# Moving an early output projection into a wait, widening narrow matmuls, splitting one load and adding fill matmuls, in a decode step that is bound by its loads

## The chip, the cores, the metric

One core of a Trainium2 chip runs the whole program. The metric is device time in microseconds (us) of one execution. The kernel before takes 672.7 us (median of three executions). A time of an execution is about 1.8 us more than the span that its profile shows, and the profile's times count from the start of the span.

Words used below: a *value unit* is one 4 MB load of the value cache (two heads of one batch) and the 32 matmuls on it; a pass is one batch, with four key units and then four value units; the *tail* is what follows the key units of the last batch. *Half clock* and *full clock* are a granted TensorE clock of 0.50 and 1.00 in the profile.

## The reference

A transformer block for one new token in each of 8 batches: adaptive layer norm, attention with 32 query heads over a cache of 8 key/value heads by 8192 positions, output projection, layer norm, MLP with squared ReLU.

```python
mod = (silu(c) @ w_mod).reshape(8, 6, 1, -1)          # sa, ca, ga, sb, cb, gb
h = layernorm(x) * (1 + ca) + sa
q = (h @ wq) ...                                       # 32 heads of 128
p = softmax(q k^T * 128**-0.5);  o = p v               # caches: 8 x 8 x 8192 x 128 bf16, twice
x = x + ga * (o @ wo)                                  # wo: 4096 x 512
h = layernorm(x) * (1 + cb) + sb
r = relu(h @ w1 + b1);  x = x + gb * ((r * r) @ w2 + b2)   # 512 x 1792, 1792 x 512
```

## The kernel before

Every large load goes through one queue, in the order of need, into a ring of four 4 MB slots. In the tail the order is: third value unit; last value unit in four pieces (2, 1, 0.5, 0.5 MB); the 1 MB of output weights that belong to the last unit; first MLP weights (1.75 MB); second MLP weights (1.5 and 0.25 MB). In all timelines below TensorE's matmuls come in the order of the program. The parts that matter, with cuts:

```python
for p in range(NP):                       # last batch: value units 0, 1, 2, then the last
    if not lastu:
        for m in range(32):  # matmul bank(p) += Pm(32 cols) x values(512 cols), 4 column groups
        ...                                # copy, 4 selecting matmuls, normalise -> oTn
    else:
        ...                                # issue loads of wo (last part), W1, W2
        # early output projection of units 0..2
        for hl in range(REP):
            for j in range(4): ...         # 16 permuting matmuls -> pP, then copied to oP
        for f in range(FT): ...            # 14 bias matmuls into hT_ps; 2 into yN_ps
        for g in range(6):
            for j in range(4):
                for k in range(KT):        # 96 matmuls, 8 moving columns each
                    op("tensor", ... e.matmul(attn_ps[:, k, :], wo_sb[:, 4*g+j, k*128:(k+1)*128],
                                              oP[:, j, g, :], ...), [t, d_woe])
        ...                                # last unit: 24 matmuls, then 2 x 16 with 8 columns ("direct")
        for x in range(8):
            for k in range(KT): ...        # last projection: 32 matmuls, waits for d_wo
...                                        # residual, layer norm (with 4 and 14 fill matmuls) -> hbT
for hh in range(2):                        # first MLP layer: 56 matmuls of 8 columns
    for f in range(7*hh, 7*(hh+1)):
        wcol = lambda k, f=f: W1v[:, k, :].rearrange("p (q f) -> p f q", f=FT)[:, f, :]   # step of 14
        for k in range(KT): ...  e.matmul(hT_ps[hh][:, f % 7, :], wcol(k), hbT[:, k, :], ...)
for f in range(FT):                        # second layer: 28 matmuls of 256 columns, wait for d_w2
    ...
```

`pe_fill(n)` issues n matmuls of 128 columns on an identity whose result nobody reads; they are meant to keep the clock up.

## Time and profile before

| | us |
|---|---|
| time, median | 672.71 |
| span of the profiled execution | 670.8 |
| last weights land (issue time plus time to landing) | about 665 |
| end of the second MLP layer | 667.9 |
| half clock in the tail | 629.6 to 633.0, 643.2 to 646.6, and from 650.05 to the end |

From the page of the kernel before: the span, then three rows of 40 equal slices (granted clock in tenths, busy share of the DMA engines in tenths, GB/s), then the bytes read.

```profile
span 670.8 us, 15868 instructions
...
PEclk9998985799869986799578987599777998699875
...
DMA  9999999999999999999999999999999999999995
...
GB/s 376 430 420 426 432 432 432 425 434 434 432 436 423 434 434 432 436 424 432 434 436 432 428 425 434 436 436 432 422 432 434 436 436 424 428 434 438 436 391 210
...
HBM read 283.66 MB, written 0.01 MB: 423 GB/s over the span
```

The DMA row is 9 from the first slice to the last but one. The program is its loads: 283.66 MB at 423 GB/s. What can shrink without fewer bytes is only what happens after the last bytes, so everything below is about the last 45 us.

The DMA view of the kernel before, for three loads of the tail (size, and us from issue to landing), and the timeline's lines of their issue (start, duration, engine, source line). Issue plus time to landing gives 656.4 us for the output weights, 660.9 for the first MLP weights and 664.5 for the larger part of the second.

```profile
wo_sb<-in_A_wo_dram SPq DMA_DIRECT2D x1, 1024.0 KB, 29.8
...
ring<-in_B_w_dram SPq DMA_DIRECT2D x1, 1792.0 KB, 24.6
...
ring<-in_B_w_dram SPq DMA_DIRECT2D x1, 1536.0 KB, 15.2
```

```profile
626.55 0.42 SPq L560 DMA_DIRECT2D wo_sb<-in_A_wo_dram  x1
...
636.33 12.95 SPq L562 DMA_DIRECT2D ring<-in_B_w_dram  x1
...
649.32 2.50 SPq L565 DMA_DIRECT2D ring<-in_B_w_dram  x2
```

The timeline of the kernel before, TensorE's lines of the tail (start us, duration us, engine, source line, operation, operands, count, and in brackets the idle time before it and what ended that).

```profile
634.38 1.91 PE L536 MATMUL PS<-ring,Pm 128*32 128x512 bf16 x32 [0.54 <-DVE rinv L517]
...
637.27 1.91 PE L536 MATMUL PS<-ring,Pm 128*32 128x512 bf16 x32
...
643.54 3.41 PE L536 MATMUL PS<-ring,Pm 128*32 128x512 bf16 x32 [3.31 <-DMA ring<-in_A_v_cache_dram]
...
648.55 1.01 PE L583 MATMUL PS<-ONE,b_row 1*128 1x8 bf16 x14
...
649.69 2.69 PE L594 MATMUL PS<-oP,wo_sb 128*128 128x8 bf16 x96
...
652.31 2.75 PE L610 MATMUL PS<-ring,Pm 128*32 128x512 bf16 x24
...
656.87 1.02 PE L627 MATMUL PS<-oTn,wo_sb 128*128 128x8 bf16 x32 [0.29 <-DVE oTn L622]
...
661.30 3.51 PE L665 MATMUL PS<-hbT,ring 128*128 128x8 bf16 x56
...
664.74 3.15 PE L676 MATMUL PS<-ring,hidT 128*8 128x256 bf16 x28
```

The first two value units take 1.91 us each, the third 3.41: that is the clock. Before the third TensorE idled 3.31 us for a load. The block of early projection (L594, 96 matmuls, 28 ns each) lies between the third and the last unit. The first MLP layer (L665) takes 63 ns for each matmul, the output projection's (L627) 32, at the same clock and of the same shape.

The clock in the same stretches, from the windows view of the kernel before (window, length, busy us and count of each engine, granted clock, DMA share, GB/s):

```profile
core 0: us, PE busy (x) PEld busy (x) DVE busy (x) ACT busy (x) POOL busy (x), PEclk, DMA share, GB/s
633.00:643.00 10.00, 4.67 (x74) 2.26 (x74) 2.47 (x8) 1.49 (x2) 0.00 (x0) 1.00 0.99 424
643.00:646.50 3.50, 2.96 (x28) 1.12 (x32) 0.00 (x0) 0.00 (x0) 0.00 (x0) 0.53 0.98 414
650.00:660.00 10.00, 8.91 (x198) 6.34 (x196) 1.96 (x8) 0.00 (x0) 0.00 (x0) 0.50 1.07 402
660.00:670.00 10.00, 7.89 (x99) 6.41 (x96) 2.30 (x9) 0.90 (x3) 0.00 (x0) 0.50 0.25 99
```

TensorE is "busy" 8.91 of 10 us from 650 to 660 and still has half the clock: 164 of the 198 matmuls in that stretch stream 8 columns.

### The profile page before, as it was taken

What the parts mean: (1) busy time and instruction counts of PE and PEld (TensorE: products, weight loads), DVE (VectorE), ACT (ScalarE), POOL (GpSimd) and SP (SyncE); (2) the same over time, 40 slices, a digit from 0 to 9 for tenths busy, and PEclk for the clock granted to TensorE, in tenths of its full rate; (3) what the DMA queues carried; (4) which work ended last, traced back from release to release, by engine and by line L of the source; (5) the groups of instructions that cost most, each with busy time, mean ns of one, the idle gap of its engine ahead of it and who ended that gap; (6) DMA issues with size and microseconds to landing.
All of it is one profiled execution on the core that took longest, in us unless ns stands there. A gap on an engine that the chain in (4) does not pass through costs nothing.

```text
span 670.8 us, 15868 instructions
## 1 busy us (share of the span) xinstructions
PE 483.1 (72%) x7332; PEld 345.3 (51%) x7332; DVE 300.2 (45%) x567; ACT 235.1 (35%) x281; POOL 17.1 (3%) x67
## 2 busy tenths in 40 slices
PE   2288853997559964698839974699637985399667
PEld 2276531875237731576318751477316762187435
DVE  2155721567126740466216661267414672166612
ACT  2044610466016630365105650166304650066500
POOL 7200000000000000000000000000000000000000
PEclk9998985799869986799578987599777998699875
DMA  9999999999999999999999999999999999999995
GB/s 376 430 420 426 432 432 432 425 434 434 432 436 423 434 434 432 436 424 432 434 436 432 428 425 434 436 436 432 422 432 434 436 436 424 428 434 438 436 391 210
DMA packets 12665, 283.95 MB, mean 423 GB/s; under 512 B 1218, under 2 KB 2275, under 8 KB 3940
## 3 DMA queue, kind: packets, MB, share of 16 engines
q1 hardware_dynamic: 12596, 283.65, 98.8%
q8 instruction: 13, 0.21, 0.1%
q14 instruction: 8, 0.07, 0.0%
q10 hardware_dynamic: 48, 0.02, 0.0%
HBM read 283.66 MB, written 0.01 MB: 423 GB/s over the span
## 4 chain that ended last, share of the span: by engine, by line
PE 55%; DMA 38%; DVE 3%; ACT 2%; issue 1%; ACTq 0%
PE PS L438 35%; DMA ring<-in_A_k_cache_dram 33%; PE PS L453 9%; DMA ring<-in_A_v_cache_dram 4%; PE PS L536 3%; PE PS L497 3%; ACT KTb L443 1%; DMA KTb<-in_A_x_dram 1%; ACT P_sb L488 1%; DVE m L458 1%; PE PS L516 1%; PE PS L665 0%; PE PS L676 0%; DVE Pm L510 0%; PE PS L610 0%
## 5 line engine op out<-in xcount | busy, mean ns | idle before, releaser
L443 ACT ACTIVATE KTb<-PS 128x1024 bf16<-128x1024 bf16 x192 | 196.5, 1024 | 368.4 <-PE PS L438 368.4
L438 PE MATMUL PS<-IDENT,ring 128*128 128x128 bf16 x4096 | 266.5, 227 | 46.6 <-DMA ring<-in_A_k_cache_dram 38.5
L438 PEld LDWEIGHTS PS<-IDENT,ring 128*128 128x128 bf16 x4096 | 245.9, 102 | 95.4 <-DMA ring<-in_A_k_cache_dram 40.0
L445 DVE COPY KTb<-PS 128x1024 bf16<-128x1024 bf16 x320 | 210.1, 687 | 145.2 <-PE PS L438 142.9
L536 PE MATMUL PS<-ring,Pm 128*32 128x512 bf16 x992 | 87.0, 513 | 61.1 <-DMA ring<-in_A_v_cache_dram 56.8
L545 DVE CAST O_sb<-PS 128x512 bf16<-128x512 f32 x31 | 21.4, 692 | 140.7 <-PE PS L536 140.7
L453 PE MATMUL PS<-KTb,Qb 128*32 128x512 bf16 x1024 | 79.2, 386 | 4.5 <-ACT KTb L443 4.5
L536 PEld LDWEIGHTS PS<-ring,Pm 128*32 128x32 bf16 x992 | 30.3, 120 | 99.1 <-DMA ring<-in_A_v_cache_dram 58.1
L497 PE MATMUL PS<-IDENT,P_sb 128*64 128x128 bf16 x512 | 26.4, 282 | 10.2 <-ACT P_sb L488 10.0
L497 PEld LDWEIGHTS PS<-IDENT,P_sb 128*64 128x64 bf16 x512 | 22.7, 150 | 12.7 <-ACT P_sb L488 12.6
L549 PEld LDWEIGHTS PS<-SEL,O_sb 128*128 128x128 bf16 x124 | 5.3, 99 | 45.9 <-DVE O_sb L545 45.9
L488 ACT ACTIVATE P_sb<-PS,negm 128x512 bf16<-128x512 f32 x32 | 21.5, 685 | 18.9 <-DVE negm L485 18.9
L510 DVE COPY Pm<-PS 64x512 bf16<-64x512 bf16 x48 | 20.2, 421 | 17.0 <-PE PS L497 15.8
L453 PEld LDWEIGHTS PS<-KTb,Qb 128*32 128x32 bf16 x1024 | 15.5, 94 | 21.1 <-ACT KTb L443 8.5
L549 PE MATMUL PS<-SEL,O_sb 128*128 128x8 bf16 x124 | 8.0, 170 | 24.8 <-DVE O_sb L545 24.8
L458 DVE TENSOR_REDUCE m<-PS 128x1 f32<-128x512 f32 x32 | 22.0, 689 | 6.6 <-PE PS L453 6.6
L507 ACT ACTIVATE Pm<-PS 64x512 bf16<-64x512 bf16 x16 | 9.5, 592 | 6.5 <-PE PS L497 6.3
L552 DVE TENSOR_TENSOR oTn<-PS,rinv 128x8 bf16<-128x8 f32 x31 | 6.0, 194 | 11.0 <-PE PS L549 11.0
L397 PE MATMUL PS<-haT,ring 128*128 128x8 bf16 x128 | 3.7, 168 | 9.2 <-DMA ring<-in_A_wq_dram 6.8
L654 ACT ACTIVATE std<-PS,epst 128x8 f32<-128x8 f32 x1 | 0.3, 267 | 25.5 <-PE PS L652 25.5
L516 PE MATMUL PS<-rhs_r,ONES 128*128 128x32 f32 x16 | 4.2, 349 | 6.8 <-DVE rhs_r L514 6.8
L483 PE MATMUL PS<-Dm,R 128*128 128x4 bf16 x8 | 1.4, 178 | 10.1 <-DVE Dm L481 10.1
(114 smaller groups left out, 105.2 us busy)
## 6 DMA issues: line engine op xcount, KB each, us to landing
ring<-in_A_k_cache_dram SPq DMA_DIRECT2D x32, 4096.0 KB, 35.0
ring<-in_A_v_cache_dram SPq DMA_DIRECT2D x31, 4096.0 KB, 28.2
ring<-in_A_wq_dram SPq DMA_DIRECT2D x1, 4096.0 KB, 20.0
ring<-in_w_mod_dram SPq DMA_DIRECT2D x1, 3072.0 KB, 10.2
wo_sb<-in_A_wo_dram SPq DMA_DIRECT2D x1, 3072.0 KB, 45.3
ring<-in_A_v_cache_dram SPq DMA_DIRECT2D x1, 2048.0 KB, 23.6
ring<-in_B_w_dram SPq DMA_DIRECT2D x1, 1792.0 KB, 24.6
ring<-in_B_w_dram SPq DMA_DIRECT2D x1, 1536.0 KB, 15.2
```

What stands on the lines that cost most here:

```text
L438: t = op("tensor", lambda e, j=j, i=i: e.matmul(STG[j][:, i, :], src[:, 32 * k + 8 * j + i, :], IDENT[:, :], is_transpose=True), [loaded[n ...
L443: stg_free[j] = op("scalar", lambda e, j=j, dst=dst: e.activation(dst, STG[j], ACT.Copy), [t], "scaP")
L445: stg_free[j] = op("vector", lambda e, j=j, dst=dst: e.tensor_copy(dst, STG[j]), [t], "vecP")
L453: t = op("tensor", lambda e, hf=hf, q=q, rhs=rhs: e.matmul(PS[32 * q:32 * (q + 1), k, :], Qb[:, 2 * p + hf, :], rhs, start=(p == 0 and hf ...
L458: return op("vector", lambda e: e.tensor_reduce(m4[:, k:k + 1], bank(k), AX.X, ALU.max), [t])
L488: exps.append(op("scalar", lambda e, k=k: e.activation(P_sb[:, k, :], bank(k), ACT.Exp, bias=negm[:, 0:1], scale=inv_sqrt, accum_out=rs4[: ...
L497: t = op("tensor", lambda e, k=k, i=i, hf=hf, src=src: e.matmul(STG[k][64 * hf:64 * (hf + 1), i, :], src, IDENT[:, :], is_transpose=True, ...
L510: done.append(op("vector", lambda e, dst=dst, frm=frm: e.tensor_copy(dst, frm), [t, k_pm], "vecP"))
L516: t = op("tensor", lambda e: e.matmul(tot_ps, ONES[:, :], rhs_r[:]), [t])
L536: t = op("tensor", lambda e, p=p, m=m, cg=cg, vt=vt, Obank=Obank: e.matmul(Obank[32 * cg:32 * (cg + 1), :], lhs[:, p, 32 * m:32 * m + 32], ...
L545: t = op("vector", lambda e, osb=osb, Obank=Obank: e.tensor_copy(osb, Obank), [t], "vecP")
L549: t = op("tensor", lambda e, i=i, osb=osb, oT_ps=oT_ps: e.matmul(oT_ps, osb[:, i * 128:(i + 1) * 128], SEL[:, i, :], start=(i == 0), stop= ...
```

## The change

Its intent: the 64 of 96 early projection matmuls that need only units 0 and 1 go into the wait for the third unit; narrow matmuls stream the same 8 columns eight times (64 columns, seven copies thrown away), which is meant to make TensorE count as active and keep its clock; first MLP weights come in two loads, so that three quarters of that layer can start earlier. Two more groups of fills come with it. The core of the diff:

```diff
+        wide = lambda ap: ap.unsqueeze(1).to_broadcast([128, 8, B])
+                    if lastb and p == 1:                 # after value unit 1, ahead of value unit 2
+                        k_oP = early(0, 2, ...)          # permuting matmuls and copy
+                        for f in range(FT): ...          # the 14 bias matmuls
+                        project(0, 2, k_oP)              # 64 matmuls
+                    if lastb and p == 2:
+                        k_oP = early(2, 3, [norm_last])
+                        ...                              # 2 bias matmuls
+                        project(2, 3, k_oP)              # 32 matmuls
-                    d_w1 = dma(... W1v ...)
+                    d_w1 = [dma(... W1v[:, a:z] ...) for a, z in ((0, 3), (3, 4))]
-   attn_ps[:, k, :], wo_sb[...], oP[:, j, g, :]
+   attn_w[:, k, :, :], wo_sb[...], wide(oP[:, j, g, :])          # likewise direct, last projection, layer 1
                     for m in range(24):
+                        if m == 16:
+                            pe_fill(12, 7)
-        for hh in range(2): ... for f ...: for k in range(KT):
+        for ks in (range(KT - 1), range(KT - 1, KT)): for f in range(FT): for k in ks:
         for f in range(FT):
+            if f == F2:
+                pe_fill(6, 7)
```

More of the change, by code (lines that the diff above doesn't have):

```diff
@@ L254, in bass_adaLN_cond__gqa_block_cached__dense_activation_squared_relu__decode_kernel @@
         sem = lambda name: E(nc.semaphore(name))
-        s_c, s_x, s_wm, s_wq, s_woe, s_wo, s_bb, s_w1 = (
-            sem(f"d_{n}") for n in ("c", "x", "wm", "wq", "woe", "wo", "bb", "w1"))
+        s_c, s_x, s_wm, s_wq, s_woe, s_wo, s_bb = (
+            sem(f"d_{n}") for n in ("c", "x", "wm", "wq", "woe", "wo", "bb"))
+        s_w1 = [sem(f"d_w1{i}") for i in range(2)]
         s_w2 = [sem(f"d_w2{i}") for i in range(2)]
@@ L458, in scores, with early, project @@
                 return op("vector", lambda e: e.tensor_reduce(m4[:, k:k + 1], bank(k), AX.X, ALU.max), [t])
+        wide = lambda ap: ap.unsqueeze(1).to_broadcast([128, 8, B])
+        attn_w = bank(4)[:, 0:64 * KT].rearrange("p (k a b) -> p k a b", k=KT, a=8)
+        attn_ps = attn_w[:, :, 0, :]
+        hT_w = [bank(i)[:, 0:64 * 7].rearrange("p (f a b) -> p f a b", f=7, a=8) for i in range(2)]
+        hT_ps = [h[:, :, 0, :] for h in hT_w]
+        yN_ps = bank(2)[:, 0:256]
+        def early(q0, q1, deps):
+            nq = q1 - q0
+            pP = bank(6)[:, 64 * q0:64 * q1].rearrange("p (j g b) -> p j g b", j=4, g=2 * nq)
+            for hl in range(REP):
+                for j in range(4):
+                    t = op("tensor", lambda e, hl=hl, j=j: e.matmul(
+                        pP[32 * hl:32 * (hl + 1), j, :, :].rearrange("p (q h) b -> p h q b", h=2),
+                        PERM[:, j, :], oTn_p[:, :, q0:q1, hl, :], start=True, stop=True,
+                        tile_position=(0, 32 * hl)), deps)
+            return op("vector", lambda e: e.tensor_copy(oP[:, :, 2 * q0:2 * q1, :], pP), [t])
+        def project(q0, q1, k_oP):
+            for g in range(2 * q0, 2 * q1):
+                for j in range(4):
+                    for k in range(KT):
+                        op("tensor", lambda e, g=g, j=j, k=k: e.matmul(
+                            attn_w[:, k, :, :], wo_sb[:, 4 * g + j, k * 128:(k + 1) * 128], wide(oP[:, j, g, :]),
+                            start=(g == 0 and j == 0 and k == 0), stop=False, skip_group_check=True),
+                            [k_oP, d_woe])
         for b in range(B):
@@ L554, in bass_adaLN_cond__gqa_block_cached__dense_activation_squared_relu__decode_kernel @@
                         [t], "vecP")
+                    if lastb and p == 1:
+                        k_oP = early(0, 2, [norm_last, k_all] + stg_free + hold)
+                        b1v = b1_row[:].rearrange("o (p f) -> o f p", f=FT)
+                        for f in range(FT):
+                            op("tensor", lambda e, f=f: e.matmul(
+                                hT_ps[f // 7][:, f % 7, :], b1v[:, f, :], ONE8[:, :],
+                                start=(f % 7 == 0), stop=False, skip_group_check=True), [d_b2, s_bank_free[f // 7]])
+                        project(0, 2, k_oP)
+                    if lastb and p == 2:
+                        k_oP = early(2, 3, [norm_last])
+                        for cc in range(2):
+                            op("tensor", lambda e, cc=cc: e.matmul(
+                                yN_ps[64 * cc:64 * cc + B, :], ONE8[:, :], b2_row[:, 256 * cc:256 * (cc + 1)],
+                                start=True, stop=False, tile_position=(0, 64 * cc), skip_group_check=True),
+                                [s_bank_free[2]])
+                        project(2, 3, k_oP)
                 else:
@@ L561, in bass_adaLN_cond__gqa_block_cached__dense_activation_squared_relu__decode_kernel @@
                         wo_sb[:, 24:32, :], A_wo[24 * DH:, :].rearrange("(h dh) n -> dh h n", dh=DH)))
-                    d_w1 = dma("sync", s_w1, lambda e: e.dma_start(W1v, B_w1.rearrange("(k p) f -> p k f", p=128)),
-                               [released[s0]])
+                    w1_r = B_w1.rearrange("(k p) f -> p k f", p=128)
+                    d_w1 = [dma("sync", s_w1[i], lambda e, a=a, z=z: e.dma_start(W1v[:, a:z], w1_r[:, a:z]),
+                                [released[s0]]) for i, (a, z) in enumerate(((0, 3), (3, 4)))]
                     w2_r = B_w2.rearrange("(p f) n -> p f n", p=128)
@@ L566, in bass_adaLN_cond__gqa_block_cached__dense_activation_squared_relu__decode_kernel @@
                             for i, (a, z) in enumerate(((0, F2), (F2, FT)))]
-                    attn_ps = bank(4)[:, 0:KT * B].rearrange("p (k b) -> p k b", k=KT)
-                    hT_ps = [bank(i)[:, 0:7 * B].rearrange("p (f b) -> p f b", f=7) for i in range(2)]
-                    yN_ps = bank(2)[:, 0:256]
-                    b1v = b1_row[:].rearrange("o (p f) -> o f p", f=FT)
-                    pP = bank(6)[:, 0:192].rearrange("p (j g b) -> p j g b", j=4, g=6)
-                    for hl in range(REP):
-                        for j in range(4):
-                            t = op("tensor", lambda e, hl=hl, j=j: e.matmul(
-                                pP[32 * hl:32 * (hl + 1), j, :, :].rearrange("p (q h) b -> p h q b", h=2),
-                                PERM[:, j, :], oTn_p[:, :, 0:NP - 1, hl, :], start=True, stop=True,
-                                tile_position=(0, 32 * hl)), [norm_last, k_all] + stg_free + hold)
@@ L581, in bass_adaLN_cond__gqa_block_cached__dense_activation_squared_relu__decode_kernel @@
-                    t = op("vector", lambda e: e.tensor_copy(oP[:], pP), [t])
-                    for f in range(FT):
-                        op("tensor", lambda e, f=f: e.matmul(
-                            hT_ps[f // 7][:, f % 7, :], b1v[:, f, :], ONE8[:, :],
-                            start=(f % 7 == 0), stop=False, skip_group_check=True), [d_b2, s_bank_free[f // 7]])
-                    for cc in range(2):
-                        op("tensor", lambda e, cc=cc: e.matmul(
-                            yN_ps[64 * cc:64 * cc + B, :], ONE8[:, :], b2_row[:, 256 * cc:256 * (cc + 1)],
-                            start=True, stop=False, tile_position=(0, 64 * cc), skip_group_check=True),
-                            [s_bank_free[2]])
@@ L591, in bass_adaLN_cond__gqa_block_cached__dense_activation_squared_relu__decode_kernel @@
-                    for g in range(6):
-                        for j in range(4):
-                            for k in range(KT):
-                                op("tensor", lambda e, g=g, j=j, k=k: e.matmul(
-                                    attn_ps[:, k, :], wo_sb[:, 4 * g + j, k * 128:(k + 1) * 128], oP[:, j, g, :],
-                                    start=(g == 0 and j == 0 and k == 0), stop=False, skip_group_check=True),
-                                    [t, d_woe])
-                    oT_ps = bank(5)[:, 0:8]
+                    oT_w = bank(5)[:, 0:64].rearrange("p (a b) -> p a b", a=8)
@@ L601, in direct @@
+                    oT_ps = oT_w[:, 0, :]
                     def direct(a, z, i, first, final):
@@ L603, in direct @@
                             t = op("tensor", lambda e, m=m: e.matmul(
-                                oT_ps, vt[:, m, :], lhs[:, NP - 1, 8 * m:8 * m + 8], start=(first and m == a),
-                                stop=(final and m == z - 1)), [loaded[n][i], k_rinv] + pmd[m // 32])
+                                oT_w, vt[:, m, :], wide(lhs[:, NP - 1, 8 * m:8 * m + 8]), start=(first and m == a),
+                                stop=(final and m == z - 1), skip_group_check=True), [loaded[n][i], k_rinv] + pmd[m // 32])
                         return t
@@ L619, in bass_adaLN_cond__gqa_block_cached__dense_activation_squared_relu__decode_kernel @@
                         op("tensor", lambda e, i=i: e.matmul(
-                            oT_ps, osb[:, i * 128:(i + 1) * 128], SEL[:, i, :], start=False, stop=False), [t, k_all])
+                            oT_ps, osb[:, i * 128:(i + 1) * 128], SEL[:, i, :], start=False, stop=False,
+                            skip_group_check=True), [t, k_all])
                     t = direct(112, 128, 3, False, True)
@@ L627, in bass_adaLN_cond__gqa_block_cached__dense_activation_squared_relu__decode_kernel @@
                             k_attn = op("tensor", lambda e, x=x, k=k: e.matmul(
-                                attn_ps[:, k, :], wo_sb[:, 24 + x, k * 128:(k + 1) * 128],
-                                oTn[:, 16 * (x // 4) + 4 * (NP - 1) + x % 4, :],
+                                attn_w[:, k, :, :], wo_sb[:, 24 + x, k * 128:(k + 1) * 128],
+                                wide(oTn[:, 16 * (x // 4) + 4 * (NP - 1) + x % 4, :]),
                                 start=False, stop=(x == 7), skip_group_check=True), [t, d_wo])
@@ L659, in bass_adaLN_cond__gqa_block_cached__dense_activation_squared_relu__decode_kernel @@
         k_sq = []
-        for hh in range(2):
-            fs = slice(7 * hh, 7 * (hh + 1))
-            for f in range(7 * hh, 7 * (hh + 1)):
-                wcol = lambda k, f=f: W1v[:, k, :].rearrange("p (q f) -> p f q", f=FT)[:, f, :]
-                for k in range(KT):
-                    t = op("tensor", lambda e, f=f, k=k, hh=hh, wcol=wcol: e.matmul(
-                        hT_ps[hh][:, f % 7, :], wcol(k), hbT[:, k, :], start=False, stop=(k == KT - 1),
-                        skip_group_check=True), [k_hb, d_w1])
-            t = op("vector", lambda e, hh=hh, fs=fs: e.tensor_scalar(rT[:, fs, :], hT_ps[hh], 0.0, None, ALU.max), [t])
-            k_sq.append(op("vector", lambda e, fs=fs: e.tensor_tensor(
-                hidT[:, fs, :], rT[:, fs, :], rT[:, fs, :], ALU.mult), [t]))
+        wcol = lambda k, f: W1v[:, k, :].rearrange("p (q f) -> p f q", f=FT)[:, f, :]
+        for ks in (range(KT - 1), range(KT - 1, KT)):
+            for f in range(FT):
+                for k in ks:
+                    t = op("tensor", lambda e, f=f, k=k: e.matmul(
+                        hT_w[f // 7][:, f % 7, :, :], wcol(k, f), wide(hbT[:, k, :]), start=False, stop=(k == KT - 1),
+                        skip_group_check=True), [k_hb, d_w1[k // (KT - 1)]])
+                if k == KT - 1 and f % 7 == 6:
+                    hh = f // 7
+                    fs = slice(7 * hh, 7 * (hh + 1))
+                    t = op("vector", lambda e, hh=hh, fs=fs: e.tensor_scalar(
+                        rT[:, fs, :], hT_ps[hh], 0.0, None, ALU.max), [t])
+                    k_sq.append(op("vector", lambda e, fs=fs: e.tensor_tensor(
+                        hidT[:, fs, :], rT[:, fs, :], rT[:, fs, :], ALU.mult), [t]))
         for cc in range(2):
```

## The prediction

> **What bounds the kernel.** The DMA queue. The page shows 283.65 MB at 423 GB/s over the 670.8 us span, and the slice rows keep DMA at 9 tenths to the last slice; the chain of waits returns to a key or value load in each pass. The change touches none of that, and moves no byte. Only the tail after the last bytes can shrink. In half-microsecond windows the DMA share fades from 661 us and is nearly zero from 664.5; by issue time plus time to landing (DMA view) the loads of the tail land at: last value unit's first chunk 648.35 us, its last about 653; output weights of the last unit 656.4; first MLP weights 660.9; second MLP weights 664.5 and 665.1.
>
> **The tail now (timeline, us from the start).** TensorE idles 640.3 to 643.5, waiting for the third value unit; runs that unit at half clock 643.5 to 647.0 (3.41; the first two took 1.91 each at full clock); norm done 648.24; early projection block (16 permuting, 14 bias, 2 bias, 96 narrow matmuls: 0.3 + 1.0 + 0.3 + 2.7) to 652.3; last unit to 656.6; its projection 656.87 to 657.9; LayerNorm to 661.0; first MLP layer 56 matmuls at 62.7 ns, 661.3 to 664.8; second layer 28 matmuls in 3.15 (half clock), to 667.9; 2.9 more to the end. The granted clock is 0.50 from 650.2 to the end.
>
> **Moves, costs.**
> - 64 of 96 projection matmuls (64 x 28 ns = 1.8 us) and 14 bias matmuls (1.0 us) go into the 3.2 us idle stretch. They fit, barely: the third unit may start 0.2 us later, but at full clock if the stretch counts as activity, saving 1.5. The chain ahead of the last unit gets about 3.5 us shorter.
> - Most of this is swallowed: the last unit waits for its chunks (to about 653.3), its projection for weights landing at 656.4. It started at 656.87, so at most 0.5 us survives there.
> - 64 columns: a narrow matmul costs 28 to 32 ns now whatever the clock. The Trainium skill (TensorE: Matmul & The Clock Gate, Part 1 and "Back-to-back issue gap") gives N/1.2 cold and N/2.4 + 2.5 ns warm: estimate 53 ns cold, 29 warm. Wide is free warm, and costs about 0.7 us per 32 cold. Its use is the clock: the page's 3.4 us activity window agrees with this trace, whose clock switches at 629.6, 633.0, 643.2, 646.65, 650.1 us. I expect TensorE warm until about 653, cold again in the wait for 656.4, so the last projection may take 1.7 instead of 1.0 us; but that density should warm the clock by 660 to 662.
> - MLP: weights split 3:1 lets 42 of 56 matmuls start near 660. Their weight loads are strided (157 ns each against 104), so warmth may help little. Second layer at full clock takes about 1.6 us instead of 3.15, but cannot finish before 665.1 plus about 0.3.
>
> **Sum.** Floor by the last landing: 665.4 + 2.9 = 668.3, 2.5 us better. With cold losses I expect TensorE done near 666.6 rather than 667.9: 1.3 us better.
>
> Predicted 671.4 us (range 670.0 to 673.0). Chances: faster by over 2% 0.01, within 2% 0.98, slower 0.01.
>
> **Right if:** the span shortens by 0.5 to 2.5 us, all after the last landing; DMA landings within 0.3 us of before; the idle stretch at 640 to 643.5 filled; third unit about 1.9 us; new TensorE waits for DMA before the last projection and second layer; second layer near 55 ns per matmul.
>
> **Wrong if:** the clock stays half in the MLP (then same time or 0.5 us slower, wide matmuls at 53 ns); DMA ends at another time; or the first layer runs much faster than 62 ns warm and reaches the floor.

## The result

672.02 us median of four executions (671.45 to 673.17) against 672.76 for the kernel before in the same rounds; ratio 0.9991, 95% interval 0.9974 to 1.0009: no difference that the measurement can tell from none. (Ratios here are the mean time of one kernel's fast runs over that of the other's of the same rounds, so not quite the ratio of the medians quoted. The ratios of the experiments below fit means that leave out the execution that was profiled; the means in the text include it.) Five more executions of the same file in the experiments below gave a mean of 673.5 us; all nine have a mean of 672.9 (4 x 672.16 + 5 x 673.49, over 9) and reach from 671.4 to 675.5, where the kernel before spreads by 1.0 us.

The timeline of the changed kernel, the lines that answer to those of before (L564 is a value unit, L483 the early projection, L627 the last unit, L431 fills, L645 the last projection, L682 and L699 the MLP layers):

```profile
634.88 3.02 PE L564 MATMUL PS<-ring,Pm 128*32 128x512 bf16 x32 [0.54 <-DVE rinv L545]
...
638.89 3.59 PE L564 MATMUL PS<-ring,Pm 128*32 128x512 bf16 x32
...
645.01 3.06 PE L483 MATMUL PS<-oP,wo_sb 128*128 128x64 bf16 x64
...
648.00 2.46 PE L564 MATMUL PS<-ring,Pm 128*32 128x512 bf16 x32
...
652.49 1.15 PE L483 MATMUL PS<-oP,wo_sb 128*128 128x64 bf16 x32 [0.17 <-DVE oP L477]
...
653.58 1.05 PE L627 MATMUL PS<-ring,Pm 128*32 128x512 bf16 x16
...
654.55 0.84 PE L431 MATMUL PS<-IDENT 128*128 128x128 bf16 x12
...
655.33 0.61 PE L627 MATMUL PS<-ring,Pm 128*32 128x512 bf16 x8
...
657.77 1.15 PE L645 MATMUL PS<-oTn,wo_sb 128*128 128x64 bf16 x32 [0.29 <-DVE oTn L640]
...
661.87 3.55 PE L682 MATMUL PS<-hbT,ring 128*128 128x64 bf16 x56 [0.25 <-DVE hbT L675]
...
665.55 1.48 PE L699 MATMUL PS<-ring,hidT 128*8 128x256 bf16 x24
...
666.96 0.51 PE L431 MATMUL PS<-IDENT 128*128 128x128 bf16 x6
...
667.40 0.39 PE L699 MATMUL PS<-ring,hidT 128*8 128x256 bf16 x4
```

The same stretch of the changed kernel in the windows view (columns as before):

```profile
635.00:642.00 7.00, 6.21 (x68) 2.29 (x60) 0.89 (x2) 0.00 (x0) 0.00 (x0) 0.54 0.98 417
646.00:649.00 3.00, 3.00 (x51) 2.36 (x52) 0.00 (x0) 0.00 (x0) 0.00 (x0) 0.50 0.96 395
658.00:670.00 12.00, 8.68 (x149) 7.16 (x145) 3.32 (x15) 0.90 (x3) 0.00 (x0) 0.99 0.38 155
```

What the reader should see:

- The clock in the MLP is at 0.99 now, where it was 0.50. The second layer's matmuls take 1.48 + 0.39 us instead of 3.15.
- The first two value units take 3.02 and 3.59 us instead of 1.91 each. They are not part of the change. The clock was at half from 635.5 to 642.3.
- So the moved block begins at 643.8 (its permuting matmuls), not near 640.5, where the profile before would have had room for it; there is no idle stretch left for it, and the third unit, which has been on chip since about 643.5, starts at 648.00 instead of 643.54.
- The end of the second layer is where it was: 667.8 against 667.9.

| start of, us | before | changed | difference |
|---|---|---|---|
| third value unit | 643.54 | 648.00 | +4.46 |
| last unit | 652.31 | 653.58 | +1.27 |
| last projection | 656.87 | 657.77 | +0.90 |
| first MLP layer | 661.30 | 661.87 | +0.57 |
| second MLP layer | 664.74 | 665.55 | +0.81 |
| final multiply on VectorE, just after it | 667.94 | 667.83 | -0.11 |

Of the 4.46 us by which the third unit is late, 3.2 are gone at the start of the last unit: 64 of the 96 early matmuls are already done, and the third unit takes 2.46 us instead of 3.41. The rest is worked off after that, most of it in the second MLP layer, where the clock is better.

### The profile page after: what moved, and what is told of

It is laid out like the page before. It is cut to its first block, busy times and chain, and to the rows that moved or that the text cites. A ratio compares the mean times of both kernels' runs of the same rounds, so it can differ in the third digit from the quotient of the medians.

```text
span 670.8 us, 15938 instructions
## 1 busy us (share of the span) xinstructions
PE 481.1 (72%) x7366; PEld 345.6 (52%) x7366; DVE 300.3 (45%) x568; ACT 235.3 (35%) x281; POOL 17.0 (3%) x67
## 4 chain that ended last, share of the span: by engine, by line
PE 57%; DMA 35%; DVE 4%; ACT 2%; issue 1%
PE PS L439 36%; DMA ring<-in_A_k_cache_dram 33%; PE PS L454 9%; PE PS L564 4%; PE PS L525 3%; DMA ring<-in_w_mod_dram 2%; ACT KTb L444 1%; ACT P_sb L516 1%; DVE m L459 1%; DVE Pm L538 1%; PE PS L544 1%; PE PS L483 1%; PE PS L682 0%; DVE rinv L545 0%; PE PS L386 0%
## 5 line engine op out<-in xcount | busy, mean ns | idle before, releaser
L564 PE MATMUL PS<-ring,Pm 128*32 128x512 bf16 x992 | 85.2, 504 | 62.7 <-DMA ring<-in_A_v_cache_dram 58.3
L564 PEld LDWEIGHTS PS<-ring,Pm 128*32 128x32 bf16 x992 | 30.1, 118 | 99.4 <-DMA ring<-in_A_v_cache_dram 59.6
L525 PEld LDWEIGHTS PS<-IDENT,P_sb 128*64 128x64 bf16 x512 | 21.0, 140 | 13.5 <-ACT P_sb L516 13.2
```

The costliest lines, as they stand in the source:

```text
L525: t = op("tensor", lambda e, k=k, i=i, hf=hf, src=src: e.matmul(STG[k][64 * hf:64 * (hf + 1), i, :], src, IDENT[:, :], is_transpose=True, ...
L564: t = op("tensor", lambda e, p=p, m=m, cg=cg, vt=vt, Obank=Obank: e.matmul(Obank[32 * cg:32 * (cg + 1), :], lhs[:, p, 32 * m:32 * m + 32], ...
```

## The experiments

Twelve kernels ran, in three groups, each timed in five rounds beside the kernel before on the same chip. Each group ran on another chip; the means of the kernel before in the three groups are 672.5, 672.7 and 672.8 us. All gave correct results.

### First group: the same again, and each idea alone

**The changed kernel again** (no edit).

> The changed kernel once more, for a second profile of it. If the phase of the clock's window against the work decides (rival: clock lottery), the stretch at half clock falls elsewhere than in the first profile (it covered the first two value units and most of the early projection, 635.5 to 642.3 and 645.9 to 649.2 us): the third value unit then starts near its landing at 643.5 instead of 648.0, the last projection waits for its weights at 656.4, and the span ends 0.5 to 1.5 us earlier than 670.8. If arrivals decide (mine), the first MLP layer takes 3.5 us in this profile too, and the time stays within 671.4 to 673.2 us.

Median 673.6 us, 671.44 to 675.49; ratio 1.0006 (0.9993 to 1.0020). The profile fell on the slowest execution, span 673.8 us. The branch that I held (arrivals decide, 671.4 to 673.2 us) missed: three of five executions lie above its range. The rival had the cause, but not the sign: the clock was at half elsewhere, and for longer. Its timeline, moved block, third unit, last unit and last projection:

```profile
645.68 3.60 PE L483 MATMUL PS<-oP,wo_sb 128*128 128x64 bf16 x64
...
649.21 2.77 PE L564 MATMUL PS<-ring,Pm 128*32 128x512 bf16 x32
...
655.54 1.90 PE L627 MATMUL PS<-ring,Pm 128*32 128x512 bf16 x16
...
660.79 1.15 PE L645 MATMUL PS<-oTn,wo_sb 128*128 128x64 bf16 x32 [0.29 <-DVE oTn L640]
```

Here half clock lasted from 630.5 to 651.0 us. The 64 wide matmuls took 3.60 us (56 ns each), the third unit started 5.7 us after its landing near 643.5, and the last projection started 4.3 us after its weights had landed (656.4). This time the lateness is not worked off.

Reading the granted clock in windows of 0.1 us gives the moments at which it switches. In the kernel before there are 45 such moments between 59.5 and 650.1 us, and divided by 3.4133 us all leave the same remainder, 1.51 to 1.53; in the profile of the changed kernel also 45, all with 0.64 or 0.65. The clock is decided on a grid of 3.413 us, and the grid's offset against the work differs from one execution to the next. This is what the Trainium skill says (TensorE: Matmul & The Clock Gate, Part 1: the window "doesn't reset when your kernel starts"); here are its consequences in one table, of all fourteen profiles (times in us):

Labels beginning with b_ are edits of the kernel before, with a_ of the changed kernel; each is an experiment below: wide (64 columns alone), best (everything together, b_ without the move), fills (the fills alone), unmoved, again, narrow, dense (another step in the weight read), warm (fills in the softmax gap), move, move_wide, nofills.

| kernel | has the move | grid offset | half clock around value units 0, 1 | third unit starts | time of that execution |
|---|---|---|---|---|---|
| before | no | 1.52 | until 632.98 | 643.54 | 672.6 |
| b_wide | no | 1.04 | until 632.50 | 643.53 | 671.14 |
| b_best | no | 1.26 | until 632.72 | 643.61 | 670.78 |
| b_fills | no | 0.20 | 631.66 to 638.49 | 643.74 | 671.74 |
| a_unmoved | no | 0.20 | 631.67 to 638.49 | 643.63 | 671.59 |
| changed | yes | 0.65 | 635.52 to 642.35 | 648.00 | 672.52 |
| a_again | yes | 2.47 | 630.52 to 651.00 | 649.21 | 675.49 |
| a_narrow | yes | 0.05 | 631.51 to 638.34 | 645.87 | 674.01 |
| a_dense | yes | 0.53 | 631.99 to 638.82 | 646.05 | 672.02 |
| a_warm | yes | 3.39 | 634.85 to 638.26 | 646.54 | 672.73 |
| b_move | yes | 0.95 | 635.83 to 642.65 | 647.04 | 673.14 |
| b_move_wide | yes | 2.54 | 630.59 to 637.42 | 646.41 | 671.13 |
| a_nofills | yes | 1.70 | until 633.16 | 643.94 | 672.03 |
| a_best | yes | 1.16 | none | 643.65 | 670.82 |

Without the move the third unit started within 0.25 us of 643.5 in all five profiles, two of them with a half-clock first unit; in these two the wait before it shrank to 0.9 us. They share one offset (0.20) and their clocks switch at the same moments of the tail, within 0.02 us. With it, in seven of nine it started 2.3 to 5.7 us late. The 3.3 us of idle time in the profile before were not spare: in other executions half-clock value units use them up.

**Narrow matmuls in the changed kernel.** All `wide(...)` operands back to 8 columns; move, split and fills kept.

> The changed kernel with 8-column matmuls again; order, split weights and fills kept. If the 64 columns buy the clock for the MLP, the clock is 0.5 from about 650 us on, the second MLP layer takes 3.1 us instead of 1.9 (fills included), and the time is about 1 us worse than the changed kernel's, near 672.8. If the moved work alone is what pays, it is as fast as the changed kernel or up to 1 us faster (no 48 ns matmuls in a cold stretch), 671.0 to 672.0. First MLP layer 3.5 us in either case.

674.11 us median, ratio 1.0020 (1.0006 to 1.0033), 0.2% slower than the kernel before, mean 673.9 against 672.9 of the changed kernel. Its second layer ran at half clock, 24 matmuls in 2.73 us against 1.48:

```profile
665.67 2.73 PE L699 MATMUL PS<-ring,hidT 128*8 128x256 bf16 x24
```

The first branch of the expectation holds in the main (the clock was at half from 658.8 us on, not from 650): the columns buy the clock of the end.

**64 columns alone on the kernel before.**

```diff
-  attn_ps[:, k, :], wo_sb[...], oP[:, j, g, :]
+  attn_w[:, k, :, :], wo_sb[...], wide(oP[:, j, g, :])      # and the other three groups; nothing else
```

> The kernel before with 64 columns only: nothing moved, one load, no added fills. If columns buy the clock, the last 12 us are at full clock, the second layer takes 1.6 us instead of 3.15, and the time is 0.5 to 1.5 us under the kernel before unless the 96 early matmuls run cold at 48 ns (2 us more ahead of the last unit, half of it swallowed by the wait for its loads). If columns do nothing, 672.7 us and the clock 0.5 as before. First MLP layer 3.5 us in either case.

671.05 us median, ratio 0.9982 (0.9968 to 0.9995): faster than before by about 1.3 us in the mean, and in the mean better than the whole change. The third unit's and the second layer's line:

```profile
643.53 3.18 PE L536 MATMUL PS<-ring,Pm 128*32 128x512 bf16 x32 [3.47 <-DMA ring<-in_A_v_cache_dram]
...
664.81 1.70 PE L681 MATMUL PS<-ring,hidT 128*8 128x256 bf16 x28
```

The second layer's 1.70 us against 3.15 are the gain. The 96 early matmuls took 4.56 us instead of 2.69 here, mostly at half clock, but the last projection began only 0.4 us later than before (657.24).

**Another step in the weight read.** Hidden units go to partitions in pairs, so that the first layer's weights are read with a step of 2 elements instead of 14, and second-layer weights come in runs of 2 KB instead of 12.

```diff
-  w2_r = B_w2.rearrange("(p f) n -> p f n", p=128)
+  w2_r = B_w2.rearrange("(g p c) n -> p g (c n)", p=128, c=2)
-  wcol = lambda k, f: W1v[:, k, :].rearrange("p (q f) -> p f q", f=FT)[:, f, :]
+  wcol = lambda k, f: W1v[:, k, :].rearrange("p (g q c) -> p g c q", q=128, c=2)[:, f // 2, f % 2, :]
```

> The changed kernel with another assignment of hidden units to partitions: weights of the first MLP layer are read with a step of 2 elements instead of 14, second-layer weights load in runs of 2 KB instead of 12 KB. If the step of the weight read sets the first layer's 63 ns per matmul (mine), it takes 56 x about 30 = 1.7 us instead of 3.5, the second layer then waits for its weights (664.5 us), and the span shortens by 1.0 to 1.8 us. If the clock or the matmul issue sets it, 3.5 us and no gain. If the shorter runs slow the loads, the last landing comes later than 665 us and eats the gain.

672.03 us median, ratio 0.9998 (0.9984 to 1.0011), mean 0.6 us under the changed kernel's nine. First and second layer in its timeline:

```profile
661.33 2.45 PE L683 MATMUL PS<-hbT,ring 128*128 128x64 bf16 x56
...
665.05 1.48 PE L700 MATMUL PS<-ring,hidT 128*8 128x256 bf16 x24 [1.26 <-DMA ring<-in_B_w_dram]
```

The first layer falls from 3.55 to 2.45 us although most of it ran at half clock (until 662.7), and what is gained turns into a wait for the second layer's weights, 1.26 us in the brackets. So the step of the read set the 63 ns. The expected 1.0 to 1.8 us of the span did not come: 0.5 between this profile and the first of the changed kernel, whose clocks differ. The shorter runs did not visibly slow the loads: from the landing of the output weights to the last landing it is 8.9 us here, 8.7 to 8.8 in the profile of the kernel before and the two of the changed kernel. At full clock the same reading takes 1.83 us (a_best below), 33 ns a matmul.

### Second group: the move, the clock and what the runs point to

**The move undone** (all 96 early matmuls again after the third unit; 64 columns, split, fills kept).

> The changed kernel with only the move undone: all 96 early matmuls again ahead of the last unit; 64 columns, split load and fills stay. Five profiles showed that the clock switches on a fixed grid of 3.413 us whose offset against the work differs by execution. If the move is what costs (new theory: in executions whose first two value units run at half clock the idle stretch is not there, and the moved block holds up the third unit, whose data has long landed), this kernel is faster than the changed one by 1 to 2 us in the mean and spreads less, near 671.2 us like the 64-columns-only kernel. If the fills or the split load cost, it stays near 673 us.

673.25 us median, ratio 1.0008 (0.9995 to 1.0022). A miss: it is not faster than the changed kernel (mean 673.0 against 672.9), so the move is not what spoils it by itself. Against the 64-columns-only kernel it has the split load and the fills more, and takes 1.7 us longer in the mean. That pointed at the fills; that the split load adds nothing that shows, the third group tells.

**Fills in the softmax gap**, to hold the clock for the value units.

```diff
             maxes = [m for m in maxes if m is not None]
+            pe_fill(16, 4)
...
+            pe_fill(20, 4)          # after the matmul that spreads the maxima
```

> The changed kernel plus 36 fill matmuls in the softmax gap of each pass, into a bank that is free there, so that the clock does not fall before the first value units. If half-clock value units are what makes the move costly, the first two units take 1.9 us each in the profile, the third starts within 0.5 us of its landing near 643.5, the last projection waits for its weights, and the time is 670.5 to 671.5 us with a spread under 1 us instead of 4. If the move is bad for another reason, 672 to 674 us with the spread kept.

671.97 us median, 671.44 to 672.73, ratio 0.9987 (0.9974 to 1.0001). A miss in the time, 0.5 us above the expected range, though the spread falls from 4 to 1.3 us: in the profile the clock still dropped, at 634.85, with value unit 0 at 3.52 us and the third unit at 646.54; value unit 1 took 1.91 us. The window before, 631.4 to 634.9, held 1.4 us of transposes, 0.4 us of a small matmul and waits; my fills lay ahead of it.

**Everything together, with the move**: softmax fills, 24 fills ahead of the last projection, step of 2, second-layer weights in three loads, no six fills in the second layer.

```diff
+  enumerate(((0, 6), (6, 10), (10, FT)))         # loads of W2, was ((0, F2), (F2, FT))
+                    pe_fill(24, 7)                # ahead of the last projection
-            if f == F2:
-                pe_fill(6, 7)
```

> All that the runs point to in one: the changed kernel with the softmax fills, 24 fills ahead of the last projection, the 2-element weight step, second-layer weights in three loads (6, 4, 4 tiles) and the six fills of the second layer gone. First layer 1.7 to 2.5 us, second layer ends about 0.5 us after the last landing near 665.1, span near 668.7, time near 670.3 us: the floor that the prediction put at 668.3 of span. If it stays above 671 us, the tail is held by something not yet seen.

670.91 us median, 670.82 to 671.04, ratio 0.9973 (0.9960 to 0.9987). Third unit, last projection, first layer, end of the second layer:

```profile
643.65 1.91 PE L566 MATMUL PS<-ring,Pm 128*32 128x512 bf16 x32 [0.85 <-DMA ring<-in_A_v_cache_dram]
...
656.64 1.14 PE L649 MATMUL PS<-oTn,wo_sb 128*128 128x64 bf16 x32 [0.99 <-DMA wo_sb<-in_A_wo_dram]
...
660.73 1.83 PE L686 MATMUL PS<-hbT,ring 128*128 128x64 bf16 x56 [0.25 <-DVE hbT L679]
...
665.55 0.60 PE L701 MATMUL PS<-ring,hidT 128*8 128x256 bf16 x8 [0.67 <-DMA ring<-in_B_w_dram]
```

Three of the four begin when a load lands, as their brackets show (the first layer waits for its input from VectorE), and the last eight matmuls start at 665.55, 0.6 us before the end of the layer. What remains is arrivals. The time is 0.6 us above what I expected: the last load landed at 665.5 us, not 665.1, and the eight matmuls come after it.

**Everything together, without the move**: the kernel before with 64 columns, step of 2 and the three loads. No move, no added fills, no split of the first weights.

> The kernel before with 64 columns, the 2-element weight step and the three loads, but neither move nor fills. If arrivals alone hold the tail, it equals the combined kernel with the move, near 670.3 us. If the move pays once its stretch is safe, it is slower than that one by up to 0.8 us: its last projection starts up to 0.8 us after the weights' landing.

670.78 us median, 670.73 to 670.92, ratio 0.9971 (0.9958 to 0.9985). It equals the other one, for its last eight matmuls wait for the same landing:

```profile
665.50 0.60 PE L682 MATMUL PS<-ring,hidT 128*8 128x256 bf16 x8 [0.68 <-DMA ring<-in_B_w_dram]
```

With the end held by arrivals, the move is worth nothing even where its stretch is safe. This is the version to keep: smaller than the change, 1.9 us under the kernel before, and all ten executions of the two combined kernels (670.7 to 671.0) lie under every one of the kernel before (672.3 to 673.3).

### Third group: the parts one by one

**The fills alone**, on the 64-columns-only kernel.

```diff
+                        if m == 16:
+                            pe_fill(12, 7)
+            if f == F2:
+                pe_fill(6, 7)
```

> The 64-columns-only kernel (671.05 us earlier) plus the change's two groups of fills (12 inside the last unit, 6 inside the second layer). If the fills run while their data has already landed, as the profiles show (last unit begun 652 to 656 us, its second chunk landed near 650.8), they lie on the critical path: 0.75 to 0.8 us and 0.44 us at full clock, more at half: 672.2 to 672.8 us. If they fill waits, 671.0 as without them.

672.8 us median, ratio 1.0001 (0.9988 to 1.0014): mean 672.62 against 671.28 without the fills, 1.3 us. The two groups of fills in its timeline:

```profile
653.84 0.84 PE L430 MATMUL PS<-IDENT 128*128 128x128 bf16 x12
...
666.29 0.51 PE L430 MATMUL PS<-IDENT 128*128 128x128 bf16 x6
```

The twelve stand inside the last unit, whose second piece had landed near 651; the six stand in the second layer at 666.3, after its last weights had landed (665). Neither fills a wait in this profile. From the start of the last unit to the start of the "direct" matmuls it is 2.30 us here and 1.41 without fills; from the start of the second layer to its end 2.24 and 1.70. That is 0.9 + 0.5 us at full clock, on the critical path.

**The changed kernel without both groups.**

> The changed kernel without both groups of fills. Fills on the critical path: 1.2 to 2 us faster than the changed kernel in the mean (its nine runs so far: mean 672.9), so about 671.4, with a spread left from the half-clock executions. Fills in waits: no change, 672.9.

672.06 us median, 671.51 to 672.22, ratio 0.9988 (0.9976 to 1.0001), mean 672.0 against 672.9 with them: 0.9 us of the expected 1.2 to 2, and 0.6 if the profiled executions (one of them at 675.49) are left out, so the time alone does not settle it. The last projection in its profile, and then, from the profile of a_best, its twelve fills and what follows them in the last unit:

```profile
656.87 1.87 PE L643 MATMUL PS<-oTn,wo_sb 128*128 128x64 bf16 x32 [2.05 <-DMA wo_sb<-in_A_wo_dram]
```

```profile
649.64 0.84 PE L431 MATMUL PS<-IDENT 128*128 128x128 bf16 x12
...
651.07 0.61 PE L630 MATMUL PS<-ring,Pm 128*32 128x512 bf16 x8 [0.59 <-DMA ring<-in_A_v_cache_dram]
```

Without fills the third unit started in time (643.94), the last projection waited 2.05 us for its weights, and its 32 wide matmuls took 1.87 us instead of 1.15. The clock had fallen before that wait, at 653.64, after a window with waits of 1.19 and 0.69 us for pieces of the last unit. In a_best, the combined kernel with the move, the third unit was in time too, and there the change's twelve fills lie in such a wait: TensorE waits another 0.59 us for the piece after them. So the same fills are free where TensorE is in time, and on the critical path where it is late, as in both profiles of the changed kernel and in b_fills. That any fills gain time is not shown: the combined kernel without added fills is as fast.

**The move alone** on the kernel before: 8 columns, one load, no fills.

> The kernel before with the move alone: 8 columns, one load, no fills. If what the move takes out of the chain is swallowed by the wait for the last unit's projection weights (landing 656.4 us), and lost where the value units run at half clock: within 0.5 us of the kernel before (672.7), not 2 us or more under it. The second layer still takes 3.1 us at half clock.

672.65 us median, 672.41 to 673.78, ratio 1.0001 (0.9988 to 1.0014). As expected: nothing.

**The move and 64 columns**, one load, no fills.

> Move and 64 columns, one load, no fills. Against 64 columns only (671.05 us) this tells what the move adds; against the changed kernel without fills, what the split load and its loop order add (expected: under 0.3 us). If the move pays: 670.3 to 670.8. If it costs in executions with half-clock value units: 671 to 672 us with a spread of 1 to 2 us.

671.85 us median, 670.99 to 673.81, ratio 0.9991 (0.9979 to 1.0003); mean 671.96 against 671.28 without the move, and equal to the 671.99 of the changed kernel without fills, from which it differs by the split load and its loop order. So the split adds nothing that shows, and the move adds spread: 2.8 us, against 1.4 for 64 columns alone. In its profile the third unit came 2.9 us late and the last projection waited 1.68 us for its weights all the same: a late third unit costs nothing as long as less than the slack of the later waits is used up.

The means, in us: before 672.5 to 672.8; 64 columns alone 671.3; fills on top of that 672.6; move and 64 columns 672.0; the change 672.9; move alone 672.9. The intervals of the ratios are about 0.13% (0.9 us) to each side, so single differences under 1 us are not settled by time alone. Settled by time are the gain of 64 columns alone (its interval ends at 0.9995), the loss when the change goes without them (its interval begins at 1.0006) and the two combined kernels. That the fills cost and that the move takes its room from late value units rests on the profiles beside the times. Not tried: a profile without the move in which both first units run at half clock.

## Why the prediction was right or wrong

The number was inside its range: 671.4 predicted with 670.0 to 673.0, measured 672.0, and the class, within 2%, was right. The expected gain of 1.3 us was not there: 0.7 in the first four executions, about zero over nine. That the number fits is in part luck: the range also holds "no change" (672.7), and one step failed and one cost was left out.

- *DMA bounds the kernel, only the tail can shrink.* Right. Landings in the changed profile: 656.4 for the output weights, 664.4 and 665.1 for the second-layer weights, as before within 0.2 us; the first three quarters of the first-layer weights at 659.7.
- *The second layer at full clock takes about 1.6 instead of 3.15.* Right in mechanism: 1.87 us for the matmuls, and the clock was up. But the six fills stand in the middle of it and add 0.5. The sum had no term for the 18 added fills at all; they cost about 1.3 us on the 64-columns-only kernel (b_fills), as much as the whole expected gain; on the change itself 0.6 to 0.9, which the times alone do not settle.
- *The moved matmuls "go into the 3.2 us idle stretch. They fit, barely"; the third unit "at full clock".* This step failed. The stretch was read from one execution. It is 3.3 us where the clock's grid lets both first units run at 1.91 us each, 0.9 with one of them at half clock (b_fills, a_unmoved), and gone in both profiles of the change; the third unit started at 648.00 and 649.21 in the two profiles. The prediction had seen the grid and the switching moments, and used them for the late part of the tail only, not for the two units ahead of the stretch.
- *Most of the shorter chain is swallowed by the wait for 656.4.* Right where the stretch existed: 2.05 us of wait before the last projection without fills, and equal times of the combined kernels with and without the move. In the changed kernel's own two profiles that wait did not appear, because TensorE was late.
- *29 ns warm and 53 ns cold for a wide matmul* (an estimate from the Trainium skill, TensorE: Matmul & The Clock Gate, "Back-to-back issue gap"). Measured 33 (2.13 us for 64 at full clock, a_best) and 56 (3.60 us for 64 at half clock, a_again), against 28 for a narrow one: wide is not quite free at full clock and twice as long at half.
- *First layer: warmth may help little.* Right: 3.51 before, 3.55 after. That it need not be 3.5 us at all, the prediction did not ask: with a step of 2 it is 1.83.
- *Split load lets 42 matmuls start near 660.* Without effect: the layer's input was ready at 661.8, after both pieces had landed. Its loop order even delays the first half's ReLU to the end of the layer.

## What to carry to other kernels

Idle time on an engine in one profile is not yet room for work: ask what ends it, and whether the work ahead of it is always that fast; work put in program order ahead of work whose data may already be there delays it (here by 2.3 to 5.7 us). Fill matmuls are free only where the next instruction waits for something that comes later, and for longer than they take at the lower clock; everywhere else they are work on the critical path, and the same place can be one in one profile and the other in another. When the loads bound the whole, look for the last landing and shorten only what comes after it: here a better clock (64 columns, 1.3 us alone), cheaper weight reads and smaller last pieces (not tried apart) gave 1.9 us, and reordering gave none.

## What the Trainium skill lacked or had wrong

- TensorE: Matmul & The Clock Gate, Part 1, has the free-running window, but speaks of its offset only for the first matmuls of a kernel. Here the clock switched 45 times in one execution, always on that grid, and executions of one file, whose profiles differ in the offset, ran 671.4 to 675.5 us.
- The same page, Part 4, says of transposes that full clock "doesn't engage" for them. In the kernel before, a run of 64 transposes alone began at half clock at 585.25 us, the clock rose to full at 588.61, and the first other matmul came at 590.50.
- The same page, "Weight-path perf modes", allows fast weight loads "packed or strided" and gives no cost of the step; other pages (SBUF — State Buffer; Advanced Engine Details and Errata, "SBUF Cachelines") speak of a penalty for wide steps, but no page gives its size for weight loads. Here 56 load-and-matmul pairs took 3.55 us at a step of 14 elements and 1.83 us at a step of 2, both at full clock.
- No page says how much of a window must be active. In the kernel before, the window 646.65 to 650.05 was busy for 2.31 of 3.40 us, mostly with matmuls of 8 to 48 columns and of a single row, and lost the clock; the window 636.4 to 639.8 was busy for 2.10 us, nearly all of it 512-column matmuls, and kept it.
